# Mirroring the later gate and value weight slices block by block on GpSimd, with the tenth block ahead of the output weights' request

## The chip, the core and the metric

The kernel runs on one core of one Trainium2 chip. The metric is the device time of one execution in microseconds; three executions of the kernel before give its median. A profiled execution of the same program gives a trace, and a page made from it. The core's engines have names that the rest of the text uses: PE is TensorE (its weight loads are listed apart, as PEld), DVE is VectorE, ACT is ScalarE, POOL is GpSimd, SP is SyncE.

## The reference

A lightweight convolution over time, with softmaxed taps per head, feeds a gated feed-forward layer:

```
w   = softmax(weight, axis=-1)                       # 8 heads, 7 taps
x_pad = six zero rows ahead of x                     # x: (8, 4096, 192)
conv[b, s, h, :] = sum_k w[h, k] * x_pad[b, s + k, h, :]   # 24 channels per head
x   = conv.reshape(32768, 192)
out = (relu(x @ w_gate) * (x @ w_val)) @ w_out       # w_gate, w_val: (192, 1536), w_out: (1536, 192)
```

Inputs and output are float32.

## The kernel before

The eight sequences are worked on in two streams (`st` 0 and 1) of four sequences each, and a unit `u` is 1024 tokens of both streams, so there are 16 units. The convolved input `xc[u]` lies with channels on partitions: 64 channels of stream 0 on partitions 0 to 63, the same 64 channels of stream 1 on partitions 64 to 127, in three chunks `c`. Because the two streams use the two halves of the partitions, every gate and value weight has to be there twice: `Wg[0:64]` and `Wv[0:64]` for stream 0, and the same numbers in `Wg[64:128]` and `Wv[64:128]` for stream 1.

For a unit and a window `w` of 512 tokens, `gate_val` (L529) goes through 12 feature blocks `f` of 128 columns. A block is six gate matmuls (three chunks, two streams) and then six value matmuls, all L542; ACT takes the relu out of PSUM (L553) and DVE multiplies it with the value product (L554) into `hT`. After the two windows of a unit, `project` (L637) multiplies `hT` with `Wo` in half passes of 48 matmuls (L571). PSUM is a pool of four tiles, all named `ps`.

How the convolved input comes about differs. For unit 0 TensorE makes it with banded matrices: `first_block` ahead of feature block 0, and `second_block` ahead of feature block 5 of the first window. For later units two "lanes" do it with per-channel taps. `lane_load` (L187) requests the tokens into `x_e` from POOL's queue, `lane_turn` (L459) has POOL copy `x_e` into `x_p` (L466, four copies a unit) and SP turn `x_p` into `x_r`, channels on partitions, by DMA transposes (L470, nine for unit 1, one after another in SP's queue: five after the first two copies, then four). From the first five, ACT makes the start of an accumulator (L502) and DVE the other taps (L516); from the last four come the products of the POOL lane (L486 on ACT, L488 on DVE), which POOL adds up (L492). A part of unit 1 is again made by TensorE: while unit 0 is projected, `project` calls two conv items, "x" and "y" (L405), which ACT copies out into the tile `y` (L430), and SP transposes.

`project` for unit 0 goes in the order half pass (0,0), x, (1,0), x, y, (0,1), y, (1,1), (2,0), then the others. In ACT's program, five L486 products for unit 1 (`fetch(0)`) stand ahead of the two copies that empty the PSUM tile of "x". The half pass (2,0) takes the PSUM tile that these two copies release, and (3,0) the one that the next eviction (L597, of (0,0) and (0,1)) releases. All engines run their instructions in the order in which the program lists them (`manual_schedule`); the order around the change is written out by hand.

The weights arrive in six column slices, `CUTS = [0, 128, 384, 640, 896, 1152, 1536]`, that is, feature blocks 0; 1, 2; 3, 4; 5, 6; 7, 8; 9, 10, 11. `load_w(s)` requests slice `s` of gate and value into partitions 0 to 63 (L159, on POOL's queue; `which` 1 is the gate alone, 2 the value alone). The other half is a copy on the chip: DVE for slices 0 and 1, POOL for the others, `pool_cols` (L177) for slice 2 and `pool_halves` (L172, recorded at L170) for slices 3, 4 and 5, each time the whole gate slice and then the whole value slice. A request on POOL's queue takes POOL's time, and POOL stands still at a copy until the slice has landed.

Three places hold the part of POOL's program that matters: after the first requests (L225 to L230), after `first_block` and the small `tap` requests (L697 to L705), and the unit loop. In between are no POOL instructions. Right after the last weight copies come the four `x_e` requests of unit 1 (L199), the copy of `tap` (L701), two `x_h` requests (L87), four memsets (L704) and the four `x_p` copies of `lane_turn(1)`.

Of the kernel before, what the change touches and what calls it, by code (L numbers as in the profile page):

```python
# [16 lines left out]
def kernel(  # L17
# [12 lines left out]
    nc = tc.nc  # L30
# [59 lines left out]
    def load_rest(steps):  # L90
        for _ in steps:
            pass
# [60 lines left out]
    Wg = const.tile([128, NCH, DFF], F16)  # L153
    Wv = const.tile([128, NCH, DFF], F16)
# [3 lines left out]
    def load_cols(src, dst, lo, hi):  # L158
        nc.gpsimd.dma_start(  # L159
            out=dst[0:64, :, lo:hi],  # L160
            in_=src.rearrange("(c p) f -> p c f", p=64)[:, :, lo:hi],
        )

    def load_w(s, which=3):
        for src, dst in ((moe_w_gate, Wg), (moe_w_val, Wv))[which == 2 : 1 + (which > 1)]:
            load_cols(src, dst, CUTS[s], CUTS[s + 1])

    def both_halves(copy, s, dst):
        cols = slice(CUTS[s], CUTS[s + 1])
        copy(out=dst[64:128, :, cols], in_=dst[0:64, :, cols])  # L170

    def pool_halves(s):  # L172
        both_halves(nc.gpsimd.tensor_copy, s, Wg)
        both_halves(nc.gpsimd.tensor_copy, s, Wv)

    def pool_cols(dst, lo, hi):
        nc.gpsimd.tensor_copy(out=dst[64:128, :, lo:hi], in_=dst[0:64, :, lo:hi])  # L177

    xes, xrs, accs, prods = {}, {}, {}, {}

# [6 lines left out]
    def lane_load(v, hold=None):  # L187


        xe = epool.tile([128, TILES, 2, NCH, 64], F16, name="x_e")  # L190
        xes[v] = xe
        for j0, n, t in pieces(v):
            bp, t0 = t // S, t % S
            start = int(t0 == 0)
            if start:
                nc.gpsimd.memset(xe[0:HALO, j0, :, :, :], 0.0)
            for st in range(2):
                b = bp + NB * st
                first = nc.gpsimd.dma_start(  # L199
                    out=xe[:, j0 + start : j0 + n, st, :, :].rearrange("p j c r -> p j (c r)"),  # L200
                    in_=bass.AP(
                        tensor=x.tensor,
                        offset=x.offset + (b * S + t0 - HALO + 128 * start) * D,
                        ap=[[D, 128], [128 * D, n - start], [1, D]],
                    ),
                )
                if hold is not None:
                    tc.add_manual_dep(first.ins, hold.ins.name, SYNC, reason="behind the turns of the lane before")
                    hold = None
                if start:  # L210
                    nc.gpsimd.dma_start(
                        out=xe[HALO:128, j0, st, :, :].rearrange("p c r -> p (c r)"),
                        in_=x[b, 0 : 128 - HALO, :],
                    )
                yield
# [5 lines left out]
    load_cols(moe_w_val, Wv, 512, 640)  # L221
    load_rest(load_x(1))
    pool_cols(Wv, 384, 512)
    pool_cols(Wg, 384, 640)
    load_w(3)  # L225
    pool_cols(Wv, 512, 640)
    load_w(4)
    load_w(5, 1)
    pool_halves(3)
    load_w(5, 2)  # L230

    ex = const.tile([H, KW + 1], FP)
# [461 lines left out]

    both_halves(nc.vector.tensor_copy, 1, Wg)
    both_halves(nc.vector.tensor_copy, 1, Wv)
    pool_halves(4)  # L697
    nc.gpsimd.dma_start(out=Wo[:], in_=moe_w_out.rearrange("(c p) d -> p c d", p=128))  # L698
    pool_halves(5)
    load_rest(lane_load(1))  # L700
    nc.gpsimd.tensor_copy(out=tap[64:128], in_=tap[0:64])  # L701
    load_rest(load_x(2))
# [69 lines left out]
```

## Time and profile before

| what | value |
|---|---|
| median of three executions | 767.84 us (766.94 to 768.06) |
| the profiled execution | 766.31 us |
| its span on the core | 764.2 us |
| granted TensorE clock | 1.0 |
| PE busy | 760.1 us, 99% of the span |
| DVE busy | 705.0 us, 92% |
| ACT busy | 600.7 us, 79% |
| POOL busy | 379.5 us, 50% |

The profiled execution took 2.1 us more than the span, which is what lies before the first and after the last recorded instruction. The times in the timelines count from the start of the span. A row of a timeline has the start, how long the instructions took, the engine, the line of the kernel, the operation, what is written from what, the shape, how many instructions were put together, and in brackets how long the engine had been idle before and what ended that. Requests of transfers on POOL are not counted as busy time, though POOL can do nothing else meanwhile; the DMA view has for each of them the bytes and the time from the start of the request to the landing.

### The profile page before, as it was taken

How to read it: one execution, taken by the hardware profiler on the slowest of the kernel's cores; microseconds unless marked ns; L12 is line 12 of the kernel's file. 1: busy time of each engine (PE TensorE's matmuls, PEld its weight loads, DVE VectorE, ACT ScalarE, POOL GpSimd, SP SyncE). 2: the span in 40 equal slices, each digit the busy share in tenths (PEclk: the TensorE clock that was granted, in tenths of full speed). 3: DMA queues.
4: the chain of work that ended last, by engine and by line, in shares of the span. 5: the costliest groups of instructions: out<-in, count | busy, mean ns of one | idle time of the engine just before them, and what ended most of it. 6: DMA issues, size and time to landing. Idle time of an engine off the chain costs nothing.

```text
span 764.2 us, 25119 instructions
## 1 busy us (share of the span) xinstructions
PE 760.1 (99%) x10935; PEld 538.1 (70%) x10935; DVE 705.0 (92%) x767; ACT 600.7 (79%) x734; POOL 379.5 (50%) x250
## 2 busy tenths in 40 slices
PE   9999999999999999999999999999999999999998
PEld 5595775957759586685866858567595775957758
DVE  7998999999999999999999999999999999999891
ACT  6787887878878787887878878787887887876571
POOL 9519448092571916629175390853909347090000
PEclk9999999999999999999999999999999999999999
DMA  9969037290452806528162281832818034220202
GB/s 118 127 109 151 5 96 81 65 114 22 94 65 85 95 24 106 49 85 95 32 110 39 85 94 44 112 23 91 88 44 131 6 98 61 64 49 17 70 1 84
DMA packets 132038, 55.93 MB, mean 73 GB/s; under 512 B 96984, under 2 KB 131928, under 8 KB 131928
## 3 DMA queue, kind: packets, MB, share of 16 engines
q1 hardware_dynamic: 90472, 38.66, 23.6%
q0 software_dynamic: 41312, 15.57, 20.6%
q8 instruction: 85, 1.39, 0.8%
q14 instruction: 25, 0.20, 0.1%
q10 hardware_dynamic: 144, 0.10, 0.0%
HBM read 31.48 MB, written 25.17 MB: 74 GB/s over the span
## 4 chain that ended last, share of the span: by engine, by line
PE 97%; POOL 2%; DMA 1%; issue 0%; ACT 0%; POOLq 0%
PE ps L542 63%; PE ps L571 32%; PE ps L620 1%; DMA Wv<-in_moe_w_val_dram 1%; DMA Wg<-in_moe_w_gate_dram 1%; POOL Wv L159 0%; POOL Wg L159 0%; POOL Wv L170 0%; POOL Wg L170 0%; POOL Wo L698 0%; POOL x_h L125 0%; POOL Wg L177 0%; POOL x_h L126 0%; PE ps L405 0%; POOL Wv L177 0%
## 5 line engine op out<-in xcount | busy, mean ns | idle before, releaser
L554 DVE TENSOR_TENSOR hT<-gr,ps 128x1024 f16<-128x1024 f16 (+1 forms) x386 | 469.1, 1216 | 36.1 <-ACT gr L553 9.1
L553 ACT ACTIVATE gr<-ps 128x1024 f16<-128x1024 f32 (+1 forms) x386 | 393.3, 1020 | 101.9 <-PE ps L542 100.0
L492 POOL TENSOR_TENSOR prods<-prods 128x1344 f32<-128x1344 f32 x70 | 212.3, 3033 | 290.2 <-DVE prods L488 265.6
L542 PE MATMUL ps<-xc,Wv 64*128 64x512 f16 x2304 | 321.1, 376 | 0.1
L542 PE MATMUL ps<-xc,Wg 64*128 64x512 f16 x2304 | 321.2, 376 | 0.0
L571 PE MATMUL ps<-Wo,hT 64*128 64x192 f16 x5952 | 249.0, 243 | 0.0
L571 PEld LDWEIGHTS <-hT 64*128 64x128 f16 x5952 | 246.8, 94 | 3.1
L542 PEld LDWEIGHTS <-Wv 64*128 64x128 f16 x2304 | 141.5, 94 | 107.9 <-issue 0.7
L542 PEld LDWEIGHTS <-Wg 64*128 64x128 f16 x2304 | 137.9, 94 | 107.6 <-issue 0.2
L516 DVE SCALAR_TENSOR_TENSOR acc<-x_r,tap,acc 128x576 f32<-128x576 f16 x225 | 165.4, 815 | 0.0
L486 ACT ACTIVATE prods<-x_r,tap 128x448 f32<-128x448 f16 x222 | 130.1, 661 | 2.1 <-DMA x_r<-x_p 2.1
L597 ACT COPY out_s<-ps 128x768 f32<-128x768 f32 (+1 forms) x64 | 45.6, 713 | 49.3 <-PE ps L571 37.2
L199 POOL DMA_DIRECT2D x_e<-in_x_dram x58 | 47.0, 821 | 14.3 <-ACT acc L502 10.9
L466 POOL COPY x_p<-x_e 128x960 f16<-128x960 f16 (+1 forms) x58 | 50.4, 908 | 1.1 <-DMA x_e<-in_x_dram 1.1
L492 POOL TENSOR_TENSOR xc<-prods 128x1344 f16<-128x1344 f32 x14 | 42.4, 3029 | 1.1
L516 DVE SCALAR_TENSOR_TENSOR xc<-x_r,tap,acc 128x576 f16<-128x576 f16 x45 | 34.1, 816 | 0.0
L502 ACT ACTIVATE acc<-x_r,tap 128x576 f32<-128x576 f16 x45 | 31.4, 765 | 0.0
L488 DVE TENSOR_SCALAR prods<-x_r,tap 128x448 f32<-128x448 f16 x70 | 26.6, 451 | 0.0
L597 DVE COPY out_s<-ps 128x384 f32<-128x384 f32 (+1 forms) x16 | 8.7, 543 | 11.6 <-PE ps L620 9.4
L620 PE MATMUL ps<-Wo,hT 128*128 128x192 f16 x96 | 8.1, 246 | 0.0
L620 PEld LDWEIGHTS <-hT 128*128 128x128 f16 x96 | 7.9, 98 | 0.2 <-issue 0.2
L145 PE MATMUL ps<-const-bfloat16-1.0 128*128 128x512 bf16 (+1 forms) x8 | 3.8, 607 | 0.8 <-PEq L756 0.8
(56 smaller groups left out, 55.9 us busy)
## 6 DMA issues: line engine op xcount, KB each, us to landing
out_dram<-out_s SPq DMA_DIRECT2D x62, 384.0 KB, 3.1
x_e<-in_x_dram POOLq DMA_DIRECT2D x34, 192.0 KB, 7.0
x_e<-in_x_dram POOLq DMA_DIRECT2D x24, 240.0 KB, 4.9
x_r<-x_p SPq DMA_TRANSPOSE x131, 4.5
Wo<-in_moe_w_out_dram POOLq DMA_DIRECT2D x1, 576.0 KB, 6.8
x_h<-in_x_dram POOLq DMA_DIRECT2D x2, 210.0 KB, 5.0
Wg<-in_moe_w_gate_dram POOLq DMA_DIRECT2D x4, 96.0 KB, 3.8
x_h<-in_x_dram POOLq DMA_DIRECT2D x2, 192.0 KB, 6.8
```

Source lines behind the costliest of these rows:

```text
L199: first = nc.gpsimd.dma_start(out=xe[:, j0 + start : j0 + n, st, :, :].rearrange("p j c r -> p j (c r)"), in_=bass.AP(tensor=x.tensor, off ...
L466: nc.gpsimd.tensor_copy(out=xp[:, j0 : j0 + n, :, st, :], in_=xe[:, j0 : j0 + n, st, :, :])
L486: engine.activation(out=out, in_=in_, func=ACTF.Copy, scale=scale)
L488: engine.tensor_scalar(out=out, in0=in_, scalar1=scale, scalar2=None, op0=ALU.mult)
L492: nc.gpsimd.tensor_tensor(out=pr[:, 0] if k < KW - 1 else xc[v + 1][:, :, LDVE:UNIT], in0=pr[:, 0], in1=pr[:, k], op=ALU.add,)
L502: nc.scalar.activation(out=accs[v][:, c, :], in_=shifted(v, c, 0, 0), func=ACTF.Copy, scale=tap[:, c, 0:1],)
L516: nc.vector.scalar_tensor_tensor(out=xc[v][:, c, 0:LDVE] if k == KW - 1 else acc[:, c, :], in0=shifted(v, c, k, 0), scalar=tap[:, c, k : k ...
L542: nc.tensor.matmul(out=pss[i][:, st, :], lhsT=W[64 * st : 64 * st + 64, c, 128 * f : 128 * (f + 1)], rhs=xcb[64 * st : 64 * st + 64, c, WI ...
L553: nc.scalar.activation(out=gr[:, sts], in_=pss[0][:, sts], func=ACTF.Relu)
L554: nc.vector.tensor_tensor(out=h[:, f, sts], in0=gr[:, sts], in1=pss[1][:, sts], op=ALU.mult)
L571: mm = nc.tensor.matmul(out=outs[q], lhsT=h[64 * r : 64 * r + 64, f, st, 128 * q : 128 * (q + 1)], rhs=Wo[64 * r : 64 * r + 64, f, :], sta ...
L597: one(out=dst[:, step * j : step * j + step], in_=src[:, step * j : step * j + step])
```

## The change

`pool_halves` goes, and `pool_blocks` comes: it copies one feature block of the gate and the same block of the value, block by block. Slices 3 to 5, six copies before (four of 768 elements per partition and two of 1152), become fourteen copies of 384. Their order among the requests also changes. Block 5 is now copied ahead of the request of the gate's slice 5, and block 6 ahead of that of the value's slice 5. Blocks 7, 8 and 9 are copied ahead of the request of `Wo`, and blocks 10 and 11 after it.

```diff
-    def pool_halves(s):
-        both_halves(nc.gpsimd.tensor_copy, s, Wg)
-        both_halves(nc.gpsimd.tensor_copy, s, Wv)
-
     def pool_cols(dst, lo, hi):
         nc.gpsimd.tensor_copy(out=dst[64:128, :, lo:hi], in_=dst[0:64, :, lo:hi])
+
+    def pool_blocks(*blocks):
+        for f in blocks:
+            pool_cols(Wg, 128 * f, 128 * f + 128)
+            pool_cols(Wv, 128 * f, 128 * f + 128)
...
     load_w(4)
+    pool_blocks(5)
     load_w(5, 1)
-    pool_halves(3)
+    pool_blocks(6)
     load_w(5, 2)
...
-    pool_halves(4)
+    pool_blocks(7, 8, 9)
     nc.gpsimd.dma_start(out=Wo[:], in_=moe_w_out.rearrange("(c p) d -> p c d", p=128))
-    pool_halves(5)
+    pool_blocks(10, 11)
     load_rest(lane_load(1))
```

The programs of the other engines keep their instructions and their order; PE gets more waits on POOL, since each block's copy now ends by itself. POOL's program after the change, from the requests of slice 4 on, is: `Wg` and `Wv` slice 4 requested; `Wg`, `Wv` block 5 copied; `Wg` slice 5 requested; block 6 copied; `Wv` slice 5 requested; blocks 7, 8 and 9 copied; `Wo` requested; blocks 10 and 11 copied; then `x_e` and the rest as before.

## The prediction, made before the changed kernel ran

> **What bounds the kernel now.** I read the page's chain first, then the timelines of POOL and of PE's weight loads around the edited copies, then the landings, and last the timelines of the engines that wait for what POOL does behind them.
>
> ```profile
> span 764.2 us, 25119 instructions
> PE 97%; POOL 2%; DMA 1%; issue 0%; ACT 0%; POOLq 0%
> ```
>
> TensorE sets the end. The other parts of the chain are the first 21.7 us, where weights arrive. So the change can gain only what PE loses to late weights, and it costs whatever it makes PE lose elsewhere.
>
> Timeline of POOL (start, us, line, what):
>
> ```profile
> 11.43 0.64 POOL L159 DMA_DIRECT2D Wv<-in_moe_w_val_dram  x1
> 12.07 0.52 POOL L177 COPY Wv<-Wv 64x384 f16<-64x384 f16 x1
> 12.51 0.64 POOL L159 DMA_DIRECT2D Wg<-in_moe_w_gate_dram  x1
> 13.14 0.63 POOL L159 DMA_DIRECT2D Wv<-in_moe_w_val_dram  x1
> 13.76 0.63 POOL L159 DMA_DIRECT2D Wg<-in_moe_w_gate_dram  x1
> 14.38 0.84 POOL L170 COPY Wg<-Wg 64x768 f16<-64x768 f16 x1
> 15.14 0.84 POOL L170 COPY Wv<-Wv 64x768 f16<-64x768 f16 x1
> 15.91 0.63 POOL L159 DMA_DIRECT2D Wv<-in_moe_w_val_dram  x1
> 16.54 0.84 POOL L170 COPY Wg<-Wg 64x768 f16<-64x768 f16 x1
> 17.61 0.82 POOL L170 COPY Wv<-Wv 64x768 f16<-64x768 f16 x1 [0.23 <-DMA Wv<-in_moe_w_val_dram]
> 18.38 1.07 POOL L698 DMA_DIRECT2D Wo<-in_moe_w_out_dram  x1
> 19.45 1.16 POOL L170 COPY Wg<-Wg 64x1152 f16<-64x1152 f16 x1
> 21.63 3.23 POOL L199 DMA_DIRECT2D x_e<-in_x_dram  x4
> 28.00 0.98 POOL L466 COPY x_p<-x_e 128x960 f16<-128x960 f16 x1 [0.33 <-DMA x_e<-in_x_dram]
> ```
>
> From start to start, a copy of 384 elements holds POOL 0.44 us (12.07 to 12.51), one of 768 holds it 0.77 (15.14 to 15.91), one of 1152 1.09 (half of 19.45 to 21.63).
>
> Timeline of PE's weight loads, blocks 8 to 10:
>
> ```profile
> 19.08 0.53 PEld L542 LDWEIGHTS <-Wg 64*128 64x128 f16 x6
> 20.38 0.09 PEld L542 LDWEIGHTS <-Wg 64*128 64x128 f16 x1
> 20.66 0.33 PEld L542 LDWEIGHTS <-Wg 64*128 64x128 f16 x5 [0.19 <-POOL Wg L170]
> 21.02 0.09 PEld L542 LDWEIGHTS <-Wv 64*128 64x128 f16 x1
> 21.74 0.33 PEld L542 LDWEIGHTS <-Wv 64*128 64x128 f16 x5 [0.62 <-POOL Wv L170]
> 21.98 0.74 PEld L542 LDWEIGHTS <-Wg 64*128 64x128 f16 x6
> ```
>
> A block starts 1.30 us after the one before (19.08 to 20.38); block 10 starts 1.60 after block 9 (20.38 to 21.98). Its second loads, those of the copied half, waited for POOL twice. So the whole loss that the change can remove is **0.30 us**, at block 9.
>
> **The change part by part.** Landings first (DMA view, one row from each of several short stretches: KB, us from the request's start):
>
> ```profile
> Wv<-in_moe_w_val_dram POOLq DMA_DIRECT2D x1, 96.0 KB, 2.9
> ...
> Wg<-in_moe_w_gate_dram POOLq DMA_DIRECT2D x1, 144.0 KB, 4.1
> Wv<-in_moe_w_val_dram POOLq DMA_DIRECT2D x1, 96.0 KB, 4.4
> ...
> Wv<-in_moe_w_val_dram POOLq DMA_DIRECT2D x1, 144.0 KB, 3.2
> ...
> Wo<-in_moe_w_out_dram POOLq DMA_DIRECT2D x1, 576.0 KB, 6.8
> ...
> x_e<-in_x_dram POOLq DMA_DIRECT2D x1, 240.0 KB, 4.8
> ...
> x_h<-in_x_dram POOLq DMA_DIRECT2D x1, 192.0 KB, 6.6
> ```
>
> *Copies.* Six copies took 4 x 0.77 + 2 x 1.09 = 5.26 us of POOL; fourteen take 14 x 0.44 = 6.16, so 0.90 us more.
>
> *Requests of slice 5.* POOL is free at 13.76. Slice 3's value was requested at 11.43 and landed 2.9 later, at 14.33; copies of block 5 therefore end about 14.82. The gate's slice 5 is requested then, 1.06 us later than before (13.76), and lands 4.1 later at most, at 18.92. That request holds POOL 0.63, block 6 holds it 0.88, and the value's slice 5 is requested at 16.33, 0.42 later than before (15.91).
>
> *Blocks 7 to 9.* Block 7's value waits for slice 4's value at most till 17.55 (13.14 + 4.4). Five further steps of 0.44, from 17.60, bring POOL to the value of block 9 at 19.36 if nothing else is late: 17.60 is the value of block 7, then both of 8 and the gate of 9. The value of block 9 needs the 144 KB request of 16.33. The two requests of that size landed in 3.2 and 4.1 us, so I take the middle, 3.65: landed 19.98, copy from 20.03, done at 20.54 (0.51, as the copy at 12.07). PE wants that half right behind the load of 21.02: the wait of 0.62 goes, and with it the 0.30 us.
>
> [...]
>
> *The `Wo` request.* It comes at 20.03 + 0.44 = 20.47 instead of 18.38: **2.09 us later**. Blocks 10 and 11 are behind it (1.07 for the request): block 10's gate is done at 22.05, while PE, at its pace of 1.30, would ask for the second half at about 21.77. With PE's loads 0.2 us ahead of their matmuls, that costs about 0.1 of the 0.30 just won.
>
> *What is queued behind it on POOL:* four `x_e` requests, now at 20.47 + 1.07 + 4 x 0.44 = 23.30 instead of 21.63 (+1.67), the copy of `tap`, two `x_h` requests, the memsets, and the `x_p` copies. `Wo`, `tap`, `x_h` and the memsets have cover: nobody asks for them before the projection of unit 0, which starts when ACT is done with the gates (41.02 in the ACT rows below), and the latest, `x_h`, landed at about 31.5 (requested behind `x_e`, 21.63 + 3.23, plus 6.6). The `x_p` copies have none, as follows. The landing times from `Wo` on grow from one request to the next (4.8 for the first `x_e`, 6.6 for `x_h`), so each transfer queues behind the one before, and the row of 28.00 shows POOL waiting for `x_e`. So `x_e` lands as much later as `Wo` starts, 2.09, and at least 1.67 later if only its own request counts. I take 2.09, because of those growing times.
>
> SP, ACT, PE and DVE (timelines; the landing from the DMA view):
>
> ```profile
> 29.01 12.91 SPq L470 DMA_TRANSPOSE x_r<-x_p  x9
> 32.95 3.77 SPq L470 DMA_TRANSPOSE x_r<-x_p  x2
> 35.47 2.55 SPq L470 DMA_TRANSPOSE x_r<-x_p  x2
> x_r<-x_p SPq DMA_TRANSPOSE x2, 4.5
> ```
>
> ```profile
> 41.02 2.10 ACT L502 ACTIVATE acc<-x_r,tap 128x576 f32<-128x576 f16 x3
> 45.25 2.90 ACT L486 ACTIVATE prods<-x_r,tap 128x448 f32<-128x448 f16 x5 [2.13 <-DMA x_r<-x_p]
> 48.06 0.83 ACT L430 CAST y<-ps 112x384 f16<-112x384 f32 x2
> 48.79 0.80 ACT L597 COPY out_s<-ps 128x768 f32<-128x768 f32 x1
> ```
>
> ```profile
> 46.97 0.35 PE L405 MATMUL ps<-x_h,band 64*128 64x192 f16 x4
> 47.14 10.09 PE L571 MATMUL ps<-Wo,hT 64*128 64x192 f16 x240
> ```
>
> The nine transposes start when the second `x_p` copy ends (28.98) and go out one behind the other, whoever is idle. ACT's products wait for the last of them: 45.25. Behind them on ACT stand the two copies that empty the PSUM tile of "x", done at 48.89. PE wants that tile for (2,0): its five half passes from 47.14 take 1.98 us each (9.9 for 240 starts), so (2,0) starts at 49.12. The cover is 0.23 us, 0.2 when I leave some hundredths for the signal (17.55 to 17.61 on POOL). Whatever delays the transposes by more than 0.2 us stops TensorE.
>
> *Sum.* Transposes +2.09, less 0.2 of cover: PE starts (2,0) **1.89 us later than before**. The 0.2 or 0.3 us won at block 9 is swallowed, because this start is set by ACT, not by when PE arrives. Next, (3,0) needs the L597 copy, 49.59 + 2.09 = 51.7, and PE comes at 53.0: covered. The first five transposes (the fifth at 35.47) land about 39.9, then 42.0 instead of 39.9; ACT's L502 slips by about a microsecond and DVE's taps by less, but their output is wanted by PE only at 57.04 + 1.89:
>
> ```profile
> 53.24 2.27 DVE L516 SCALAR_TENSOR_TENSOR xc<-x_r,tap,acc 128x576 f16<-128x576 f16 x3
> ```
>
> (done 55.5). The later units' lanes move with PE. PE never waits again in the chain, so there is nothing in which the loss could be regained. The profiled execution (766.31) becomes 768.2; the median stands 1.53 above it, so 767.84 + 1.89 = **769.7 us**.
>
> Bounds: landing 3.2 and only the request counting gives 16.33 + 3.2 + 0.05 + 0.44 = 20.02 for `Wo`, `x_e` +1.22, PE +1.0. Landing 4.4, the longest weight row, gives `Wo` at 21.22, 2.84 later, PE +2.6.
>
> **The rivals.**
>
> *Not slower: the release isn't late.* If the nine transposes follow one another faster once `x_e` and `x_h` are no longer landing beside them, or ACT's wait at 45.25 has another cause, the 2.09 shrinks below 0.5, and block 9's gain stays: 767.84 - 0.3 = 767.5. For it: the fourth transpose started at 32.95 and the fifth only at 35.47, twice the usual step, so there is some slack in the train. Against it: that is 1.2 us at most, and the wait on ACT names the transposes. It decides from the point where the train makes up 1.9 us.
>
> *Smaller: the value of slice 5 lands early.* Then `Wo` goes out at 19.80, 1.42 later, and PE loses 1.2: 769.0. The 3.2 row is close to this (`Wo` at 20.02, PE +1.4); the 4.1 and 4.4 rows speak against it.
>
> *The block 10 wait alone.* Copies behind `Wo` come later than PE asks. With the longest landing, block 10's gate is done at 22.8 against 21.77, some 0.8 us of loss against 0.3 won: 768.3, if nothing of the lane shows. It also holds the case that block 9 gains nothing.
>
> **How the numbers follow.** What a measurement of this kernel can tell from no change is about 0.2%, 1.5 us. The forecast's mechanism with more than that has 0.62, since both its middle and the longer rows pass 1.5; the early landing 0.18; the hidden release 0.12; block 10 alone 0.08. The last three stay mostly within 0.2%. A gain of more than 1.5 us has no source in the trace but the scatter of runs, 0.04, out of the hidden release. So slower 0.62, same 0.34, faster 0.04. The forecast's own range is 769.0 to 770.5 (+1.2 to +2.6). With about 0.6 us for the scatter of the runs (766.94 to 768.06), and down to the early landing and block 10, it is 768.0 to 771.2, which leaves out the hidden release and little else.
>
> **What would show it.** In the profile after: block 10's loads 1.3 us behind block 9's, and no wait for POOL at block 9; `Wo` requested near 20.5; the second `x_p` copy near 30.1; the transposes from 31.1; ACT's L486 starting near 47.3; and an idle stretch of nearly 2 us on PE ahead of an L571 row, released by ACT's L430. It is wrong if PE's half passes still run without a gap, if `Wo` goes out before 19.5, or if a gap comes at another place.

## The result, and the profile after

| kernel | median (lowest to highest), runs | ratio, 95% interval |
|---|---|---|
| before, beside the changed one | 767.43 us (765.76 to 771.47), 18 | |
| changed | 771.18 us (766.88 to 775.22), 18 | 1.0049 [1.0029, 1.0069] |

The changed kernel is slower by 3.75 us at the median. Its runs spread over 8 us, and the mean granted clock of an execution, 1.0 in the shortest, is 0.998 or 0.996 in 11 of the 18. The profiled execution happens to be one of the short ones, 767.54 us with a span of 765.5. One execution of f1, a run further down, had a mean granted clock of 0.851 and took 881.94 us; no count or median of the text holds it. The lines of the changed kernel from `pool_blocks` on are numbered one or two higher than before: L573 is the half passes (L571 before), L488 ACT's products (L486), L432 the copies out of the conv items' tiles (L430).

POOL's timeline in that execution:

```profile
17.43 0.63 POOL L159 DMA_DIRECT2D Wv<-in_moe_w_val_dram  x1
20.63 0.50 POOL L173 COPY Wv<-Wv 64x384 f16<-64x384 f16 x1 [0.28 <-DMA Wv<-in_moe_w_val_dram]
21.09 1.08 POOL L700 DMA_DIRECT2D Wo<-in_moe_w_out_dram  x1
23.95 3.23 POOL L200 DMA_DIRECT2D x_e<-in_x_dram  x4
30.46 1.92 POOL L468 COPY x_p<-x_e 128x960 f16<-128x960 f16 x2 [0.30 <-DMA x_e<-in_x_dram]
```

Everything is there: block 9's value waits for its slice, `Wo` goes out 2.71 us later than before (18.38), `x_e` 2.32 later (21.63), and the second `x_p` copy 2.46 later (28.00). Not all of it is the change: this execution was already late ahead of the first changed instruction, where POOL waited 1.78 us for a gate slice (0.42 before). TensorE was late, too:

```profile
5.80 2.75 PE L367 MATMUL ps<-band,x_h 110*32 110x104 f16 x118 [0.32 <-DMA x_h<-in_x_dram]
48.30 10.18 PE L573 MATMUL ps<-Wo,hT 64*128 64x192 f16 x240
```

```profile
46.70 2.90 ACT L488 ACTIVATE prods<-x_r,tap 128x448 f32<-128x448 f16 x5 [2.42 <-DMA x_r<-x_p]
```

The five half passes begin at 48.30 instead of 47.14, because the first conv block ran late and slowly: its 120 matmuls took from 5.21 to 8.55 us here, and to 7.15 in the trace of before. ACT's products begin 1.45 us later than before (45.25). So TensorE came to half pass (2,0) almost as late as its tile did: 10.18 us for 240 matmuls instead of 10.09, 0.09 us of stop. An execution in which TensorE comes on time must show more. That is what the second trace of the same kernel was for.

### The profile page after: what moved, and what is told of

Its sections match the earlier page's. It is cut to its first block, busy times and chain, and to the rows that moved or that the text cites. A ratio compares the mean times of both kernels' runs of the same rounds, so it can differ in the third digit from the quotient of the medians.

```text
span 765.5 us, 25127 instructions
## 1 busy us (share of the span) xinstructions
PE 761.3 (99%) x10935; PEld 526.8 (69%) x10935; DVE 704.8 (92%) x767; ACT 600.4 (78%) x734; POOL 380.7 (50%) x258
## 4 chain that ended last, share of the span: by engine, by line
PE 99%; DMA 1%; issue 0%; ACT 0%; POOL 0%; POOLq 0%
PE ps L544 65%; PE ps L573 32%; PE ps L622 1%; DMA x_h<-in_x_dram 1%; PE ps L367 1%; PE ps L407 0%; ACT acc L599 0%; POOL steps L124 0%; POOLq L124 0%; POOLq L758 0%
## 5 line engine op out<-in xcount | busy, mean ns | idle before, releaser
L544 PE MATMUL ps<-xc,Wg 64*128 64x512 f16 x2304 | 317.6, 376 | 0.0
L544 PE MATMUL ps<-xc,Wv 64*128 64x512 f16 x2304 | 317.3, 376 | 0.0
L573 PE MATMUL ps<-Wo,hT 64*128 64x192 f16 x5952 | 249.0, 243 | 0.0
L573 PEld LDWEIGHTS <-hT 64*128 64x128 f16 x5952 | 246.6, 94 | 3.4
L544 PEld LDWEIGHTS <-Wv 64*128 64x128 f16 x2304 | 138.0, 94 | 111.2 <-issue 0.8
L544 PEld LDWEIGHTS <-Wg 64*128 64x128 f16 x2304 | 128.4, 94 | 116.3 <-issue 0.3
L488 ACT ACTIVATE prods<-x_r,tap 128x448 f32<-128x448 f16 x222 | 130.1, 660 | 2.4 <-DMA x_r<-x_p 2.4
L504 ACT ACTIVATE acc<-x_r,tap 128x576 f32<-128x576 f16 x45 | 31.4, 765 | 0.0
L173 POOL COPY Wg<-Wg 64x384 f16<-64x384 f16 (+1 forms) x8 | 4.4, 552 | 1.8 <-DMA Wg<-in_moe_w_gate_dram 1.8
```

The costliest lines, as they stand in the source:

```text
L488: engine.activation(out=out, in_=in_, func=ACTF.Copy, scale=scale)
L504: nc.scalar.activation(out=accs[v][:, c, :], in_=shifted(v, c, 0, 0), func=ACTF.Copy, scale=tap[:, c, 0:1],)
L544: nc.tensor.matmul(out=pss[i][:, st, :], lhsT=W[64 * st : 64 * st + 64, c, 128 * f : 128 * (f + 1)], rhs=xcb[64 * st : 64 * st + 64, c, WI ...
L573: mm = nc.tensor.matmul(out=outs[q], lhsT=h[64 * r : 64 * r + 64, f, st, 128 * q : 128 * (q + 1)], rhs=Wo[64 * r : 64 * r + 64, f, :], sta ...
```

## The experiments

Each is compared with runs of the kernel before on the same chip: e1 to e4 with 29 of them, e5 to e8 with 35, f1 to f3 with 27 and g1 with 14. Their medians are 767.13, 767.17, 767.28 and 767.25. The last column counts the executions whose mean granted clock was 0.998 or less.

| run | median us | ratio, 95% interval | low clock |
|---|---|---|---|
| kernel before (all four groups) | 767.1 to 767.3 | | 10 of 105 |
| changed kernel, first 18 runs | 771.18 | 1.0049 [1.0029, 1.0069] | 11 of 18 |
| e1, the changed kernel again | 773.08 | 1.0067 [1.0040, 1.0093] | 6 of 6 |
| e2, tiles of the conv items emptied first | 768.59 | 1.0006 [0.9989, 1.0023] | 0 of 12 |
| e3, `Wo` ahead of block 9 | 771.37 | 1.0039 [1.0015, 1.0062] | 7 of 12 |
| e4, before with `Wo` late | 767.20 | 1.0002 [0.9986, 1.0018] | 1 of 12 |
| e5, before with `x_e` 0.88 late | 767.84 | 1.0020 [0.9998, 1.0042] | 3 of 12 |
| e6, `Wo` behind `x_e` | 769.14 | 1.0026 [1.0005, 1.0046] | 4 of 12 |
| e7, changed, unit 2's `x_e` held longer | 767.24 | 0.9992 [0.9979, 1.0005] | 0 of 11 |
| e8, PE kept busy in the stop | 769.89 | 1.0037 [1.0014, 1.0060] | 3 of 12 |
| f1, before, unit 2's `x_e` held longer | 767.51 | 0.9996 [0.9981, 1.0011] | 0 of 11 |
| f2, before, unit 2's `x_e` not held | 767.06 | 0.9992 [0.9979, 1.0005] | 0 of 12 |
| f3, slice 5 requested early | 770.49 | 1.0040 [1.0020, 1.0059] | 6 of 10 |
| g1, changed, unit 2's `x_e` not held | 768.45 | 1.0012 [0.9998, 1.0026] | 0 of 11 |

**e1: the changed kernel again.** No edit.

> The changed kernel once more, for its spread and for a trace of another execution. Release theory (the later Wo request makes x_e, the transposes and ACT's copies out of the PSUM tile of conv item x late, so that TensorE stops ahead of half pass (2,0)): a gap on PE at about 49 to 51 us, of 1 to 2 us when PE came there on time, and less the later PE came; the executions that take 3 us and more over the kernel before show a granted clock under 1 in a stretch behind that gap. Rival (the first feature block runs late and cold in some executions, with no link to the change): gaps and slow matmuls only before 10 us, none at 49 to 51.

The profiled execution took 770.4 us (span 768.3). What PE waited for, from the view of waits (sum, times, longest):

```profile
PE ps L573 <- ACT y L432: 3.0, 1, 3.0
```

Timelines of POOL, ACT and PE of the same execution:

```profile
20.32 1.08 POOL L700 DMA_DIRECT2D Wo<-in_moe_w_out_dram  x1
23.20 3.23 POOL L200 DMA_DIRECT2D x_e<-in_x_dram  x4
29.96 1.85 POOL L468 COPY x_p<-x_e 128x960 f16<-128x960 f16 x2 [0.59 <-DMA x_e<-in_x_dram]
42.26 3.20 POOL L200 DMA_DIRECT2D x_e<-in_x_dram  x4 [9.11 <-ACT acc L504]
```

```profile
48.18 2.90 ACT L488 ACTIVATE prods<-x_r,tap 128x448 f32<-128x448 f16 x5 [5.48 <-DMA x_r<-x_p]
50.99 0.83 ACT L432 CAST y<-ps 112x384 f16<-112x384 f32 x2
```

```profile
46.74 2.15 PE L573 MATMUL ps<-Wo,hT 64*128 64x192 f16 x48
51.87 9.44 PE L573 MATMUL ps<-Wo,hT 64*128 64x192 f16 x192 [2.98 <-ACT y L432]
```

This is the predicted stop, released by the predicted instruction, and (2,0) starts at 51.87, 2.75 us later than the 49.12 of before. Then two things that the prediction did not have. First the chain that ended last in this execution:

```profile
40.83 1.25 SPq L472
42.09 0.04 issue
42.13 5.95 DMA x_r<-x_p
```

The last transpose is requested at 42.13 and lands 5.95 us later, where 4.5 was read before. In the kernel before, its request stands at 40.66:

```profile
40.66 1.26 SPq L470 DMA_TRANSPOSE x_r<-x_p  x1
```

In e1, between the request at 42.13 and its landing, at 42.26, POOL requests unit 2's `x_e`, 864 KB. That request is held by ACT's L504 (the accumulator, which needs the first five transposes only), so it comes when it came before (42.34), while the last transposes come later. Second, the clock. The columns are the busy time of PE, PEld, DVE, ACT and POOL in each stretch, then the granted clock, the DMA share and GB/s:

```profile
50.00:51.00 1.00, 0.00 (x0) 0.00 (x0) 1.00 (x2) 1.00 (x3) 0.00 (x0) 1.00 0.27 41
51.00:52.00 1.00, 0.13 (x3) 0.13 (x4) 1.00 (x2) 1.00 (x4) 0.00 (x0) 0.64 0.00 0
52.00:53.00 1.00, 1.00 (x16) 1.00 (x15) 1.00 (x3) 1.00 (x3) 0.00 (x0) 0.50 0.00 0
53.00:54.00 1.00, 1.00 (x17) 1.00 (x14) 1.00 (x2) 1.00 (x4) 0.00 (x0) 0.50 0.46 149
54.00:55.00 1.00, 1.00 (x20) 1.00 (x18) 1.00 (x2) 1.00 (x3) 0.00 (x0) 0.65 0.77 244
55.00:56.00 1.00, 1.00 (x30) 1.00 (x26) 1.00 (x4) 1.00 (x3) 0.00 (x0) 1.00 0.00 0
```

About 0.6 us before the stop ends, the clock falls to half: 0.72 us of it in the stretch from 51, two whole stretches, and 0.70 in the one from 54, 3.42 us together (0.36 and 0.35 divided by 0.5). The view counts 16 or 17 matmuls in a stretch at half clock, and 30 in the first one at full clock (a matmul that reaches over the edge of a stretch counts on both sides). The four half passes take 9.44 us; e6, below, shows the same 192 matmuls at full clock in 8.10, so the drop costs 1.34. With 2.75 that is 4.09, and the span is 4.1 longer than before (768.3 and 764.2).

**e2: the conv items' tiles emptied first.** The L504-held load stays; ACT's `fetch(0)` moves behind the copies out of "x" and "y".

```diff
-                elif t == 0:
-                    fetch(0)
                 done[i] = conv_turn_of(2, t, at[i], turn, done.get(i))
                 if turn:
                     conv_out(2, t, at[i], y)
+                    if t == 1:
+                        fetch(0)
```

> The changed kernel, with ACT's five products fetch(0) moved behind the copies that empty the PSUM tiles of the conv items x and y, so that these no longer stand behind the wait for the transposes. Release theory: PE has no gap at 49 to 51, and the time is that of the kernel before, 767 to 768, with the small spread of before. Rival (early part): the time and the spread of the changed kernel stay, a median near 771.

No execution has a low clock, and none is above 769.7: without the wait ahead of L432 the long stop is gone, although the last transpose lands as late as in e3 (6.4 us after its request). The median of 768.59 lies 0.6 us above the expected 767 to 768. PE's waits in this trace show a smaller stop of another kind, where SP's marks of a finished turn stand in SP's queue behind the transposes:

```profile
PE ps L573 <- SPq L586: 0.4, 1, 0.4
PE ps L407 <- SPq L420: 0.2, 1, 0.2
```

**e3: `Wo` ahead of block 9.**

```diff
-    pool_blocks(7, 8, 9)
+    pool_blocks(7, 8)
     nc.gpsimd.dma_start(out=Wo[:], ...)
-    pool_blocks(10, 11)
+    pool_blocks(9, 10, 11)
```

> The changed kernel, with the request of Wo put back ahead of block 9 (blocks 7 and 8, then Wo, then 9, 10 and 11). Release theory: Wo goes out about 1.2 us earlier than in the changed kernel, at about 19.3, so the transposes are about 0.9 later than in the kernel before, and the time lies 0.5 to 1 over it, at 768 to 768.5. Rival (splitting the copies itself, or the early part, costs the time): a median near 771 as for the changed kernel.

A miss: 771.37, as the changed kernel. POOL's timeline says why:

```profile
19.42 1.08 POOL L700 DMA_DIRECT2D Wo<-in_moe_w_out_dram  x1
23.20 3.23 POOL L200 DMA_DIRECT2D x_e<-in_x_dram  x4
30.23 1.87 POOL L468 COPY x_p<-x_e 128x960 f16<-128x960 f16 x2 [0.99 <-DMA x_e<-in_x_dram]
```

`Wo` is early, `x_e` is not, and the second `x_p` copy comes with `x_e`. Against the kernel before, `Wo` is 1.04 us later, `x_e`'s request 1.57 and that copy 2.23. So the prediction's reading that the start of `Wo` sets the landing of `x_e` falls; e5, below, shows that `x_e`'s own request does most of it. PE stopped for 2.96 us in this trace (released by L432), and the clock was low for 3.42 us again.

**e4: the kernel before with `Wo` late.** Slice 5 is copied as block 9, then `Wo`, then blocks 10 and 11 together.

```diff
     pool_halves(4)
+    pool_cols(Wg, 1152, 1280)
+    pool_cols(Wv, 1152, 1280)
     nc.gpsimd.dma_start(out=Wo[:], ...)
-    pool_halves(5)
+    pool_cols(Wg, 1280, 1536)
+    pool_cols(Wv, 1280, 1536)
```

> The kernel before, its slices copied in halves, with only the request of Wo moved behind the copies of block 9 (slice 5 is then copied as block 9 and blocks 10 and 11 together). Release theory: Wo goes out about 1 us later than before (two copies of 0.44), the transposes 1 us later, PE +0.8: 768.2, and more where the clock drops. Rival (it is the moved requests of slice 5 or the small copies): as the kernel before, 767.4.

A miss for the release theory, 767.20: the late `Wo` by itself costs nothing that can be measured, which agrees with e3 from the other side. But the traced execution of e4 (768.07 us) is one in which POOL also waited longer for slices (1.34 and 0.89 us, where the kernel before waited 0.42 and 0.23), and there `x_e` is as late as in e1:

```profile
23.36 3.23 POOL L199 DMA_DIRECT2D x_e<-in_x_dram  x4
50.91 8.10 PE L571 MATMUL ps<-Wo,hT 64*128 64x192 f16 x192 [0.81 <-ACT y L430]
```

PE stops for only 0.81 us, and the clock stays at 1.0. ACT's accumulator was 0.80 us late too (41.82 and 41.02), so unit 2's load came at 43.14, 0.55 us behind the last transpose, which landed after 4.5 us. A late `x_e` alone is not the whole loss; e7 shows the rest.

**e5: the kernel before with `x_e` late.**

```diff
     pool_halves(5)
+    extra = const.tile([64, 2, NCH, 128], F16)
+    for n in range(2):
+        nc.gpsimd.tensor_copy(out=extra[:, n], in_=Wg[0:64, :, 1408:1536])
     load_rest(lane_load(1))
```

> The kernel before, with two more copies of 384 elements on POOL (into a tile nobody reads) between the last weight copy and the x_e requests: 0.88 us, about what the fourteen small copies add. The request of Wo and the slices are untouched. If the request of x_e itself sets when x_e lands: the transposes are 0.9 later, PE stops ahead of (2,0) by 0.7 and more, and part of the executions fall into the group with a clock of 0.998, a median of 768 to 771. If Wo's start sets it (Wo's bytes run ahead of x_e's and keep the engines full): the time of the kernel before, 767.1, with its spread.

The median moves little (767.84, just under the expected 768 to 771), but 3 of 12 executions have the low clock and take 771.8 to 774.2. The trace, of an execution without the drop, has the delay by itself:

```profile
18.53 1.07 POOL L698 DMA_DIRECT2D Wo<-in_moe_w_out_dram  x1
22.80 3.23 POOL L199 DMA_DIRECT2D x_e<-in_x_dram  x4
29.38 1.92 POOL L466 COPY x_p<-x_e 128x960 f16<-128x960 f16 x2 [0.48 <-DMA x_e<-in_x_dram]
```

`Wo` is 0.15 us later than before, `x_e`'s request 1.17, the second `x_p` copy 1.38, and PE stops for 0.58 us. With 0.88 us the kernel stands near the edge; the changed kernel with its longer delay goes over it in 17 of 24 executions.

**f3: the slice 5 requests back in their old places.**

```diff
     load_w(4)
-    pool_blocks(5)
     load_w(5, 1)
-    pool_blocks(6)
+    pool_blocks(5, 6)
     load_w(5, 2)
```

> The changed kernel with the requests of slice 5 back in their old places (the gate's ahead of the copies of blocks 5 and 6, the value's behind both); small copies and the late Wo stay. If the late request of slice 5 is what pushes x_e over the edge: x_e goes out about 0.4 us earlier, and fewer executions collide, a median of 767.5 to 769. If the fourteen small copies and Wo are enough: as the changed kernel, 771 and more.

770.49, 6 of 10 with the low clock. In the trace `x_e` is not earlier (24.09), since POOL now waits 0.53 us for the value's slice 5. Neither putting these requests back (f3) nor putting `Wo` back (e3) makes the difference; what e3 and f3 share with the changed kernel are the fourteen small copies, and e4, which has only two of them, stays with the kernel before. That it is the copies is an exclusion: no run has the new order with the six old copies. The trace also shows a shorter stop that was followed by the drop:

```profile
52.03 9.75 PE L572 MATMUL ps<-Wo,hT 64*128 64x192 f16 x192 [2.25 <-ACT y L431]
53.00:54.00 1.00, 1.00 (x22) 1.00 (x17) 1.00 (x3) 1.00 (x5) 0.00 (x0) 0.60 0.29 94
54.00:55.00 1.00, 1.00 (x18) 1.00 (x14) 1.00 (x2) 1.00 (x3) 0.00 (x0) 0.50 0.92 300
55.00:56.00 1.00, 1.00 (x17) 1.00 (x14) 1.00 (x3) 1.00 (x3) 0.00 (x0) 0.50 0.00 0
56.00:57.00 1.00, 1.00 (x21) 1.00 (x19) 1.00 (x4) 1.00 (x3) 0.00 (x0) 0.69 0.00 0
```

PE stood still for 2.25 us and went on at 52.03; the clock fell only at 53.2, again for 3.42 us, and the 192 matmuls took 9.75 us instead of 8.10.

**e7: unit 2's `x_e` held behind the last transposes.** In the changed kernel, the load is now released by ACT's first product, which waits for the last transposes. `product` and `fetch` return their instructions for it, and the earlier call goes.

```diff
-                load_rest(lane_load(2, begun))
...
                 elif t == 0:
-                    fetch(0)
+                    load_rest(lane_load(2, fetch(0)[0]))
```

> The changed kernel, with the x_e requests of unit 2 held by ACT's first product, which waits for the last transpose, instead of by ACT's first accumulator instruction. If the last transposes land late (about 6 us after their request instead of 4.5) because they run into these 864 KB: the landing goes back to about 4.5, ACT's products start 1 to 1.5 us earlier, PE's stop is 1 to 2 us instead of 3, fewer executions show a lower clock, a median of 768 to 769.5. If not: as the changed kernel, 771 to 773.

All the loss is gone, more than the expected 768 to 769.5: 767.24, eleven executions between 765.89 and 768.22, none with a low clock. Nothing was made earlier on POOL; its timeline even has `Wo` at 21.19 and `x_e` at 24.06 in this execution, and the transposes start at 31.68. But they land:

```profile
x_r<-x_p SPq DMA_TRANSPOSE x8, 2.7
```

```profile
46.08 2.90 ACT L488 ACTIVATE prods<-x_r,tap 128x448 f32<-128x448 f16 x5 [2.42 <-DMA x_r<-x_p]
```

```profile
47.68 10.19 PE L573 MATMUL ps<-Wo,hT 64*128 64x192 f16 x240
```

The first of these rows is the DMA view from 34 to 50 us, with the median landing. In e3 the same row for the last transposes, from 40 us on, has 6.2 (e7's from 40 us on is again 2.7, and its very last transpose lands after 3.1):

```profile
x_r<-x_p SPq DMA_TRANSPOSE x3, 6.2
```

The transposes of e7 started 0.43 us later than e3's (31.68 and 31.25), and ACT's products came 2.8 us earlier (46.08 and 48.88). PE has no stop ahead of (2,0). So the delay that reaches TensorE is mostly the slow landing beside unit 2's load.

The other traces order in the same way. The last transpose landed 8.61 us after its request where unit 2's load was requested 0.44 us ahead of it (e8); after 5.50 to 6.4 us where the load came 0.1 to 0.44 us behind it (e1, e2, e3, e6, f3); after 3.7 to 4.5 us where it came 0.55 to 1.7 us behind (the kernel before, e4, e5, and the first trace of the changed kernel); and after 3.0 or 3.1 us where it came more than 4 us behind (f1, e7). So the 4.5 us of the kernel before already held a part of this meeting.

**e8: PE kept busy in the stop.**

```diff
             if turn == 0:
+                if (u, i) == (0, 2):
+                    for n in range(32):
+                        nc.tensor.matmul(
+                            out=at[1][0][:, n % 2, 2 * D : 512],
+                            lhsT=busy[:, 0:128],
+                            rhs=busy[:, 0 : 512 - 2 * D],
+                            start=True, stop=True, skip_group_check=True,
+                        )
                 at[i] = slots()
```

> The changed kernel with 32 matmuls of 128 columns on constants (into columns of a PSUM tile that are not read) on PE just ahead of half pass (2,0), about 2 us of work put into the stop. If the clock drop behind the stop is a cost of its own (half speed for about 3.4 us): (2,0) starts when ACT lets it, as in the changed kernel, the clock stays at 1.0, and the time falls by about 1.5 us, to 769.5. If the drop costs nothing of its own, or the stop isn't there: the time of the changed kernel, or up to 2 us more.

769.89, near the expected 769.5 and 1.3 us under the first 18 runs of the changed kernel, and 3 of 12 with a low clock instead of 17 of 24. The profiled execution is one of the three, with a stop so long that 2 us of work don't fill it:

```profile
49.96 2.06 PE L677 MATMUL ps<-const-bfloat16-1.0 128*128 128x128 bf16 x32
55.09 5.13 PE L573 MATMUL ps<-Wo,hT 64*128 64x192 f16 x80 [3.07 <-ACT y L432]
```

That the drop is a cost of its own is shown by e1's 9.44 and f3's 9.75 against 8.10. That work in the stop avoids it is only suggested by the counts: no trace shows a stop that the work filled, the changed kernel itself was not run beside it, and two of e8's executions without a low clock still took 771.87 and 772.67 us.

**e6: `Wo` behind `x_e`.**

```diff
-    pool_blocks(7, 8, 9)
-    nc.gpsimd.dma_start(out=Wo[:], ...)
-    pool_blocks(10, 11)
+    pool_blocks(7, 8, 9, 10, 11)
     load_rest(lane_load(1))
+    nc.gpsimd.dma_start(out=Wo[:], ...)
```

> The changed kernel with the request of Wo moved behind the four x_e requests (blocks 7 to 11, then x_e, then Wo). POOL saves Wo's 1.07 ahead of x_e and the transfers of x_e no longer run behind the 576 KB of Wo, about 3 us at 190 GB/s. Release theory: the transposes end earlier than in the kernel before, PE never stops at (2,0), the gain at block 9 stays: 766.8, no execution above 768.5. Rival (the small copies themselves cost the time): about 771.

A miss, 769.14. `x_e` is requested at 22.02 and the transposes start at 30.07, 0.9 earlier than in e1, but now `Wo` is requested only at 25.23, so that its transfer (6.8 us from request to landing in the kernel before) runs beside them:

```profile
30.07 14.16 SPq L472 DMA_TRANSPOSE x_r<-x_p  x9
```

They take 14.16 us to go out (12.91 in the kernel before, 13.09 in e1), the last ones meet unit 2's load again, and PE stops:

```profile
51.68 8.10 PE L573 MATMUL ps<-Wo,hT 64*128 64x192 f16 x192 [2.60 <-ACT y L432]
```

This stop of 2.60 us left the clock at 1.0 (8.10 us for 192 matmuls).

**f1 and f2: the kernel before with the load held longer, and not at all.** f1 has e7's edit; f2 has `lane_load(2)` in place of `lane_load(2, begun)`.

> The kernel before with the hold of e7 (x_e of unit 2 behind ACT's first product). If the collision of the last transposes with x_e of unit 2 is what makes a few executions of the kernel before slow (771 to 773 in 7 of 64 so far): none above 768.5, and the median as before, 767, since the others don't collide. Against e7 it shows what the changed copies are worth once nothing collides: the step at block 9 would make e7 0.3 us faster, which this cannot resolve.

> The kernel before with no hold on x_e of unit 2: its requests go out as soon as the x_p copies of unit 1 are done, near 32 us, on top of the transposes. Collision theory: the transposes land late by 3 us and more although Wo, the slices and the x_e of unit 1 are where they were; PE stops at (2,0) by 3 us or more with a clock under 1 behind it, 771 to 775. Rival (what is late is the start of the transposes alone, and it isn't late here): 767.

f1 came out as expected: 0 of 11 executions with a low clock where the kernel before has 10 of 105 (with so few runs that is no more than a hint). f2 is a miss: no execution suffers. Its load of unit 2 is requested at 30.60, moves beside the first transposes, and is all but through when the last one is requested at 40.27; that one lands after 3.0 us, and ACT's products start at 43.42 without waiting. So in f2 the early load does no harm. It does in the traces in which it is in flight as the last transposes land (3.7 to 8.61 us after their request).

**g1: the changed kernel without the hold.**

> The changed kernel with no hold on x_e of unit 2, as f2 has it for the kernel before. If only what is still being moved when the last transposes go out matters (in f2 the early 864 KB are through by 40 us and the last products of ACT start at 43.4): the products start within 46, PE does not stop at (2,0) or by less than 1 us, the clock stays at 1.0, 766.8 to 767.6, none above 769. If a late start of the transposes is enough by itself: a gap of 1 to 2 us stays, 768.5 to 770.

A partial miss: no low clock, but 768.45. Here the load is requested at 33.57, three microseconds later than in f2, and the transposes stretch to 15.09 us; ACT doesn't stop PE any more, SP does:

```profile
46.60 0.50 PE L407 MATMUL ps<-x_h,band 64*128 64x192 f16 x8 [1.92 <-SPq L420]
```

Of these kernels none is measurably faster than the kernel before; e7 and f2 come out equal to it, both 0.9992 [0.9979, 1.0005].

## Why the prediction was right, and where it was mis-sized

The direction and the path were right. That the number agrees is partly luck: the median of 771.18 lies at the very top of the forecast's 768.0 to 771.2, e1's six executions have 773.08, and all 24 executions of the changed kernel together 771.85. Two costs were missing from the sum, the later landing and the half clock, and executions like the profiled one, in which TensorE was late by itself, made up for a part of them.

- *TensorE bounds the kernel, and the change can win 0.30 us at block 9.* Right. In e1's trace of weight loads block 9 does not wait, block 10 starts 1.30 us behind it, and its second loads wait 0.28 us, which its matmuls don't feel:

```profile
20.30 0.53 PEld L544 LDWEIGHTS <-Wg 64*128 64x128 f16 x6
21.60 0.09 PEld L544 LDWEIGHTS <-Wg 64*128 64x128 f16 x1
21.97 0.33 PEld L544 LDWEIGHTS <-Wg 64*128 64x128 f16 x5 [0.28 <-POOL Wg L173]
```

PE starts the half pass ahead of (2,0) 0.40 us earlier than before (46.74 and 47.14), of which 0.08 were there ahead of block 9. None of it shows in the time of the changed kernel.
- *The copies, the landing and the requests.* Right in form (from 17.60 to 19.36 are four steps of 0.44, not five; the sum is right). The value's slice 5 landed 3.1 us after its request in one trace (17.43) and 3.4 in the other, not 3.65. e1 has `Wo` at 20.32 (predicted 20.47), `x_e` at 23.20 (23.30), the second `x_p` copy at 29.96 (30.1).
- *`x_e` lands later because `Wo` starts later.* Wrong as a cause. e4 delays `Wo` and costs nothing, e3 restores it and gains nothing; in e5 `x_e`'s own request, pushed by 0.88 us of copies, moves the `x_p` copy with `Wo` in its place. The prediction had this as its lower bound (+1.67) and chose the other. That its 2.09 comes near e1's 1.96 for the start of the transposes (30.97 and 29.01) is luck: `x_e` was requested 1.57 us later and took 0.39 longer.
- *Transposes, ACT's products, the tile of "x", (2,0).* Right, shown by the releaser in e1, e3 and e6, and by e2, which takes the tile out of this chain and with it the long stop. The cover of 0.2 us was real: in e1 the products are 2.93 us late and (2,0) 2.75.
- *The size of the stop, 1.89.* Too small: (2,0) started 2.75 us late in e1. The term that was mis-sized is the landing of the last transpose, carried over as 4.5 us; it was 5.95, since the transposes now meet unit 2's load, whose request stayed where it was. e7 shows it by taking the meeting away. The other terms were smaller than forecast: the transposes began 1.96 us later instead of 2.09, and their train made up another 0.49, so that the last request came 1.47 us later (42.13 and 40.66). With 1.45 from the landing that is 2.92 for ACT's products, and 0.2 of cover less leaves the measured 2.75.
- *What follows a stop.* The prediction took the stop as the whole cost. The clock fell to half for 3.42 us, 1.34 us more in e1. The two missing terms together are 0.86 + 1.34 = 2.20, and 1.89 + 2.20 = 4.09, e1's loss. The median of the first 18 runs, +3.75, mixes executions with this loss and ones with little, as the profiled one, in which TensorE was late by itself.
- *The rivals.* A hidden release can be had in at most the four of 24 executions that took less than 768 us; seven kept the full clock, but two of these took 769.55 and 772.56 us. In the one of the four that was traced, ACT's products were 1.45 us late, and TensorE's own lateness hid that, not a faster train; the 0.49 us that the train made up in e1 is the slack this rival counted on, and too little. The early landing (`Wo` at 19.80 is 19.36 + 0.44) played no part in the traces, and for block 10 there is at most PE's wait for a gate copy on POOL, 0.3 us in e2's and 0.5 in e7's.

Open: how a load slows transposes that were requested before it was not resolved below the level of landings. Why executions differ ahead of the first changed instruction is not known. The executions of 773 to 775 us, with clocks of 0.996, left no trace; by the clock they have the time of two such drops (one takes 0.002 off a mean over 768 us, an estimate from the 3.42 us). Nor did the one of 772.56 us with the full clock. What decides, besides the length of a stop, whether the clock falls is not known either.

## What to carry to other kernels

A request that moves on one queue takes the requests behind it along, but not those that another engine releases (in e1 `x_e` of unit 1 went out 1.57 us later, and unit 2's load at 42.26, as before at 42.34): look for transfers that are held by something that did not move, and ask whether they now meet. A short wait can cost TensorE nothing (0.28 us of a weight load in e1), while of the five stops of 2.25 us and more that were traced here four cost a stretch at half clock besides the wait, so the longest stop in the spread matters more than the mean. Where the margin is a fraction of a microsecond, several traces and the clock of each run say more than one profiled execution.

## What the hardware showed that was not expected

The clock fell with stops of 2.96 to 3.07 us (e1, e3, e8) and with one of 2.25 (f3), but not with one of 2.60 (e6), so the length of the stop alone doesn't decide. Nor does the clock fall at a fixed point of the stop: in e1 it fell 0.6 us before PE went on, in f3 1.2 us after. At the start of the kernel, TensorE ran slowly with a granted clock of 1.00 in the view: from 6 to 7 us the view counts 60 matmuls in the changed kernel's profiled execution and 88 in that of before. It is not the change that does this: the first conv block, whose matmuls these are, ends at 8.55 us in the changed kernel's execution, and the first changed instruction, POOL's copy of block 5, starts at 15.02.

```profile
6.00:7.00 1.00, 1.00 (x60) 1.00 (x55) 0.50 (x2) 0.12 (x1) 1.00 (x3) 1.00 1.32 144
```

And a load of 864 KB slowed a DMA transpose that was requested ahead of it: with the load 0.13 us behind, the transpose landed after 5.95 us (e1), with the load 4.8 us behind after 3.1 (e7). In e8, with the load 0.44 us ahead, it took 8.61.
